# Transposing V as 32-bit words: four FP32 transposes per PSUM bank in place of eight BF16 ones, in the backward half of an attention block

## The chip, the cores and the metric

The kernel runs on one core of a Trainium2 chip. That core has five engines with their own instruction queues: TensorE (PE in the profile, with its weight loads shown as PEld), VectorE (DVE), ScalarE (ACT), GpSimd (POOL) and the queue that issues nearly all DMAs (SP). All DMAs share 16 DMA engines. The metric is the time of one execution in device microseconds, as a median of several runs.

## The reference, cut to what matters

The reference is one decode step of a transformer block and its gradients. Batch 4, 32 heads, 4096 cached positions, head size 128, so there are 128 (batch, head) pairs, called heads here; each head's K and V are 4096 x 128 BF16 values, 1 MB each.

```python
# forward: h = x + attention(layernorm(x)); out = h + swiglu(layernorm(h))
scores = jnp.einsum("bhqd,bhkd->bhqk", q, k_cache) * (Dh ** -0.5)
p = softmax(scores)
o = jnp.einsum("bhqk,bhkd->bhqd", p, v_cache)
# returned: out, and by jax.vjp the gradients of x, k_cache, v_cache, wq, wo, w1, w3, w2
```

For one head, with dO the gradient of o (128 values), the backward half needs three things:

- grad V, which is the outer product of p (4096) and dO (128): 1 MB written;
- dP, which is V times dO: 4096 numbers. This is the only use of V in the backward half, and V is read from memory a second time for it;
- dS = p * (dP - c) * scale, with c one number per head, and grad K, which is the outer product of dS and q: 1 MB written.

## The kernel before, in words

**Buffers.** SBUF holds an arena of 23 slots of 4160 BF16 values per partition. A slot holds one head's K, V, grad K or grad V, or a helper. Two adjacent slots hold a pair of heads. Which slot is given to what is decided when the program is written out, by the order of the calls and the ages of the slots, so it does not depend on the times. Every engine's instruction order is the order of the calls, written by hand (`manual_schedule`); only semaphores wait.

**Stages.** Up to about 690 us the forward half streams K and V once. Around 690 to 703 us lies a middle part with few heads' work (the gradient of the SwiGLU, then dO of the first eight head groups). Then come 32 single heads (`SP = 32`), and after them the other 96 heads as 48 pairs (`NT`). Each loop iteration calls `front` (V to dP), `more_V` (grad V, running ahead), `grad_K` or `grad_pair` (grad K) and `side` (a generator with the small gradients and dq). `front` runs L = 5 heads, or LP = 3 pairs, ahead of the grad K that needs its result.

**V to dP, single heads (`front`, L1214).** V lies in SBUF as 32 blocks j (one key each) of 128 values on each partition. A contraction over the 128 values of d needs d on the partitions, so V is transposed: per group g of eight blocks, TensorE writes eight 128 x 128 BF16 transposes into one PSUM bank (`V_T`, L800), and ScalarE copies the bank back over V (L801). Two such banks (`psT`) take turns. Then eight matmuls (L1230) with 512 moving columns each, four side by side on column strips of 32, multiply the transposed V with a stationary window of `zd`, a nearly empty tile with dO in one column; four heads share one PSUM tile `dP`, each writing its own rows. GpSimd places dO into `zd` two heads ahead (`dO_window`, L1195). After every fourth head, ScalarE copies dP out (`rows_out`, L1205), TensorE transposes it with four 128 x 128 FP32 transposes (`rows_T`, L1212), and VectorE forms dS (`group_dS`, L1247 and L1250).

**Pairs.** A pair's V is loaded as one 2 MB transfer. The first half of every partition's values goes through TensorE like a single head (`front_pair`, L1322, L1323, matmuls L1337, dO placed by `dO_pair`, L1292, into `zt`). The second half is transposed on VectorE in 32 x 32 blocks of 32-bit words (`rest_pair`, L1343), and its matmuls (L1349) read every second BF16 value, since a word holds two neighbouring d. Their stationary comes from `dO_quad` (L1312, GpSimd). `group_dS_pair` makes dS of four heads from both halves (L1359 to L1372).

**Outer products and stores.** VectorE makes each outer product (L806 for one head, L1424 for a pair), and the SP queue stores it (L817, L1257, L1434). `P_pairs` (L1200) and `P2_pair` (L1421) on GpSimd copy p into doubled form for them. SP also issues the V loads (L833 single, L1282 pairs), in program order, each waiting for its slot.

Of the kernel before, what the change touches and what calls it, by code (L numbers as in the profile page):

```python
# [9 lines left out]
FP32 = mybir.dt.float32  # L10
BF16 = mybir.dt.bfloat16
# [10 lines left out]
SP = 32  # L22
# [5 lines left out]
def kernel(  # L28
# [22 lines left out]
    nc = tc.nc  # L51
# [740 lines left out]

    def V_T(s, ps, part=range(SJ // GW)):
        if s not in VTs:
            VTs[s] = V2s.pop(s)
        v = VTs[s].heads()
        for g in part:
            pt = ps.tile([P, GW, P], BF16, tag="tps", name="pt_tps")
            for i in range(GW):
                nc.tensor.transpose(pt[:, i, :], v[:, g * GW + i, :], ident_b[:])  # L800
            nc.scalar.copy(out=v[:, g * GW:(g + 1) * GW, :], in_=pt[:])  # L801
# [163 lines left out]
    with ExitStack() as c2:  # L965
# [221 lines left out]
        zd = [bw3.tile([P, 136], BF16, name=f"zd{i}", tag=f"zd{i}", bufs=1) for i in range(B)]  # L1187
        dOp = bw3.tile([P, 4, (NH - SP) // 2], BF16, name="dOp", tag="dOp", bufs=1)
        quads = bw3.tile([P, 4], BF16, name="quads", tag="quads", bufs=1)
        for i in range(B):  # L1190
            nc.gpsimd.memset(zd[i][:], 0.0)

        def dO_window(s):
            if s < SP:
                nc.gpsimd.tensor_copy(out=zd[s % B][:, 32:132:67], in_=dOT_bf[:, s:s + 1].to_broadcast([P, 2]))  # L1195
# [18 lines left out]
        def front(s):  # L1214
# [8 lines left out]
            VT = VTs[s].heads()  # L1223
# [3 lines left out]
            for u in range(2):  # L1227
                for c in range(4):
                    j0 = 8 * c + 4 * u
                    nc.tensor.matmul(rows["acc"][32 * c:32 * (c + 1), :], lhsT=zq_window(zd[hl], 2 * hl + u),  # L1230
                                     rhs=VT[:, j0:j0 + 4, :], start=(hl == 0 and u == 0),
                                     stop=(hl == B - 1 and u == 1), tile_position=(0, 32 * c))
# [8 lines left out]
        def group_dS(g):  # L1241
            i0 = g * B
            T = rows.pop("T").rearrange("p jj (c m) -> p c m jj", c=4)
            t = rows.pop("t")[:, 0:B * SJ].rearrange("p (b j) -> p b j", b=B)
            t5 = t.rearrange("p b (c u jj) -> p b c u jj", c=4, u=2)
            for hl in range(B):
                nc.vector.tensor_scalar(out=t5[:, hl], in0=T[:, :, 2 * hl:2 * hl + 2, :], scalar1=c_rep[:, i0 + hl:i0 + hl + 1],  # L1247
                                        scalar2=scale, op0=ALU.subtract, op1=ALU.mult)
# [40 lines left out]
        def dO_pair(t):  # L1289
            if t < NT:  # L1290
                s, s2 = two(t)
                nc.gpsimd.tensor_copy(out=zt[t % B][:, 32:34], in_=dOT_bf[:, s:s2 + 1:B])  # L1292

        def dO_quads():
# [11 lines left out]
            for z in zd:  # L1306
                nc.gpsimd.memset(z[:], 0.0)

        def dO_quad(t):
            if t < NT:  # L1310
                for k in range(2):
                    nc.gpsimd.tensor_tensor(out=zd[2 * (t % 2) + k][:, 3:131].rearrange("p (q c) -> p q c", c=32)[:, :, 16:24:4],  # L1312
# [3 lines left out]
        def front_pair(t, mid):  # L1316
            pl = t % 2
            v = pV[t].t[:, 0:2 * SJ * Dh].rearrange("p (j d) -> p j d", d=Dh)
            for g in range(SJ // GW):
                pt = psT.tile([P, GW, P], BF16, tag="tps", name="pt_tps")  # L1320
                for i in range(GW):
                    nc.tensor.transpose(pt[:, i, :], v[:, g * GW + i, :], ident_b[:])  # L1322
                nc.scalar.copy(out=v[:, g * GW:(g + 1) * GW, :], in_=pt[:])  # L1323
# [9 lines left out]
            for u in range(2):  # L1333
                m = 4 * pl + 2 * u
                for c in range(4):
                    j0 = 8 * c + 4 * u
                    nc.tensor.matmul(rows["acc"][32 * c:32 * (c + 1), :], lhsT=zt[t % B][:, 32 - m:64 - m], rhs=v[:, j0:j0 + 4, :],  # L1337
                                     start=(pl == 0 and u == 0), stop=False, tile_position=(0, 32 * c))

        def rest_pair(t):  # L1340
# [4 lines left out]
            for g in range(2):  # L1345
                for r in range(2):
                    for k in range(2):
                        z0 = 3 + 4 * k - 2 * pl - g
                        nc.tensor.matmul(rows["acc"][:], lhsT=zd[2 * pl + r][:, z0:z0 + P], rhs=v5[:, 16 * g:16 * (g + 1), r, :, k],  # L1349
# [6 lines left out]
        def group_dS_pair(g):  # L1356
            T = rows.pop("T").rearrange("p jj (c z l u a) -> p z l a c u jj", c=4, z=4, l=2, u=2, a=2)
# [4 lines left out]
            t5 = t[:, :, 0:SJ].rearrange("p l (c u jj) -> p l c u jj", c=4, u=2)  # L1362
            t4 = t[:, :, SJ:2 * SJ].rearrange("p l (g j) -> p l g j", g=2)
            for l in range(2):
                for a, s in enumerate(two(2 * g + l)):
                    r_ = slice(64 * a, 64 * (a + 1))
                    nc.vector.tensor_scalar(out=t5[r_, l], in0=T[r_, 0, l, a], scalar1=c_rep[r_, s:s + 1],
                                            scalar2=scale, op0=ALU.subtract, op1=ALU.mult)
                    nc.gpsimd.tensor_scalar(out=t4[r_, l], in0=R[r_, 16 + 2 * l:18 + 2 * l], scalar1=c_rep[r_, s:s + 1],  # L1369
# [4 lines left out]

        Pp, zt, P2b, dSt = {}, [], [], []
# [4 lines left out]
        def P_rows(q):  # L1380
            if q >= NT // B or q in Pp:
                return
            if not Pp:
                Pp["s"] = Slot("Pp")
                x = Pp["s"].t[:, NT * 2 * SJ:]
                zt.extend(x[:, 66 * i:66 * (i + 1)] for i in range(B))
                nc.gpsimd.memset(x[:, 0:66 * B], 0.0)
                P2b.extend(x[:, n:n + 4 * SJ].rearrange("p (j t) -> p j t", t=2) for n in (66 * B, 66 * B + 4 * SJ))
                n = 66 * B + 8 * SJ
                dSt.append(x[:, n:n + 8 * SJ].bitcast(FP32))  # L1390
# [89 lines left out]

        for s in range(2):
            dO_window(s)
# [12 lines left out]
        for s in range(SP):  # L1495
# [11 lines left out]
            elif (s + L - SP) % 2 == 0:  # L1507
                if s + L == SP:
                    dO_pair(0)
# [66 lines left out]
```

## Time and profile before

| what | value |
|---|---|
| time, median of 3 runs (lowest to highest) | 1694.92 us (1694.87 to 1697.38) |
| the profiled execution: its own time | 1696.35 us |
| its span (first to last instruction) | 1694.5 us |
| mean granted TensorE clock | 0.832 of full speed |
| bytes moved by DMA | 707.25 MB, mean 417 GB/s |
| busy: DVE, PE, ACT, POOL | 80%, 71%, 46%, 32% |
| L800, BF16 transposes of single heads | 1024, 84.3 us busy |
| L1322, BF16 transposes of pairs | 1536, 160.6 us busy |
| copies of transposed banks (L801, L1323) | 128 of 1026 ns, 192 of 1024 ns |

A busy share is an average over stages that have different limits, so the stage must be looked at on its own. In a list of waits, a line names who waited, for whom, the sum in us, how often, and the longest. Times of matmuls overlap, since a matmul starts before the one ahead of it has ended: eight of 0.22 us can take 0.6 us together.

### The profile page before, as it was taken

Reading aid. Unit: us, or ns where it says so; the run is one execution under the profiler, and the core shown is the slowest. Engines: PE = TensorE matmul, PEld = TensorE weight load, DVE = VectorE, ACT = ScalarE, POOL = GpSimd, SP = SyncE. Lnnn points to the kernel's source line nnn. Section 1 sums busy time; section 2 is a strip of 40 time slices with the busy share of each in tenths; the row PEclk is TensorE's granted clock in tenths of the full one; section 3 lists DMA queues with packets and bytes.
Section 4 is the critical chain, followed back from the end, with each engine's and each line's share of the span. In section 5 each row is a group of like instructions: output and inputs, shape, how many; then the busy total and the mean of one; then the engine's idle time right before and its main releaser. Section 6 shows DMA issues by size and latency. Waiting matters only on the chain.

```text
span 1694.5 us, 34930 instructions
## 1 busy us (share of the span) xinstructions
PE 1204.6 (71%) x14708; PEld 859.8 (51%) x14708; DVE 1347.7 (80%) x1271; ACT 780.1 (46%) x1300; POOL 538.5 (32%) x779
## 2 busy tenths in 40 slices
PE   5989888888888888878886746656565575575550
PEld 4777766677676766656664533433232333233230
DVE  5999899999999997667767779698677687587585
ACT  3455444454455544677764333434342443344330
POOL 1211223222222222223331436454353345154110
PEclk9999999999999999799879668776667666656675
DMA  9999999999999999999999999999999999999997
GB/s 402 424 424 424 424 424 425 423 424 423 414 424 413 424 412 397 393 412 425 425 426 428 429 420 429 430 429 431 430 427 431 429 413 430 430 410 429 409 382 299
DMA packets 80988, 707.25 MB, mean 417 GB/s; under 512 B 8748, under 2 KB 12984, under 8 KB 15296
## 3 DMA queue, kind: packets, MB, share of 16 engines
q1 hardware_dynamic: 80416, 704.94, 99.1%
q8 instruction: 115, 1.88, 0.4%
q14 instruction: 41, 0.34, 0.0%
q0 software_dynamic: 416, 0.10, 0.0%
HBM read 422.59 MB, written 282.34 MB: 416 GB/s over the span
## 4 chain that ended last, share of the span: by engine, by line
DMA 35%; DVE 8%; ACT 4%; PE 4%; issue 3%; POOL 1%; DVEq 0%; SPq 0%; POOLq 0%; ACTq 0%
DMA out_dram<-arena 34%; DVE arena L1424 6%; ACT arena L801 4%; DMA arena<-in_A_v_cache_dram 2%; PE pt_tps L800 1%; DVE arena L1343 1%; PE dq_ps L1000 1%; PE dP_ps L1230 1%; DVE arena L806 1%; POOL arena L1369 1%; PE pt_wo L610 0%; DVEq L1571 0%; PE rep_ps L1179 0%; PE pt_tps L1322 0%; PE dP_ps L1349 0%
## 5 line engine op out<-in xcount | busy, mean ns | idle before, releaser
L472 PE MATMUL M_ps<-arena 128*128 128x130 bf16 x4096 | 284.7, 222 | 48.9 <-DMA arena<-in_A_v_cache_dram 48.4
L457 DVE TENSOR_TENSOR arena<-arena 128x4096 bf16<-128x4096 bf16 x128 | 292.4, 2284 | 23.5 <-POOL arena L453 23.5
L1323 ACT COPY arena<-pt_tps 128x1024 bf16<-128x1024 bf16 x192 | 186.2, 1024 | 245.5 <-PE pt_tps L1322 245.3
L1424 DVE TENSOR_TENSOR arena<-dS,arena 128x8192 bf16<-128x8192 bf16 x48 | 211.5, 4408 | 100.1 <-DMA out_dram<-arena 100.1
L472 PEld LDWEIGHTS <-arena 128*128 128x128 bf16 x4096 | 250.8, 99 | 70.9 <-DMA arena<-in_A_v_cache_dram 65.1
L1322 PE MATMUL pt_tps<-ident_b,arena 128*128 128x128 bf16 x1536 | 160.6, 280 | 157.2 <-DMA arena<-in_A_v_cache_dram 135.2
L1424 DVE TENSOR_TENSOR arena<-arena 128x8192 bf16<-128x8192 bf16 x48 | 212.2, 4421 | 57.3 <-DMA out_dram<-arena 57.3
L364 DVE STREAM_TRANSPOSE arena<-arena 128x512 f32<-128x512 f32 (+1 forms) x321 | 250.5, 797 | 0.0
L1312 POOL TENSOR_TENSOR zd<-dOp,quads 128x8 bf16<-128x8 bf16 x96 | 151.1, 1589 | 268.6 <-PE dP_ps L1349 266.5
L1322 PEld LDWEIGHTS <-arena 128*128 128x128 bf16 x1536 | 139.6, 130 | 188.1 <-DMA arena<-in_A_v_cache_dram 151.4
L359 ACT COPY arena<-pt_tps 128x1024 bf16<-128x1024 bf16 x128 | 129.4, 1012 | 194.1 <-PE pt_tps L358 154.9
L1349 PE MATMUL dP_ps<-arena,zd 128*128 128x512 bf16 x384 | 145.7, 545 | 83.4 <-DVE arena L1343 83.3
L453 POOL COPY arena<-P_all 128x64 bf16<-128x64 bf16 x128 | 32.4, 253 | 412.4 <-ACT P_all L447 409.4
L370 POOL TENSOR_TENSOR W<-qrep,wmask 128x128 bf16<-128x128 bf16 x128 | 119.5, 933 | 86.5 <-PE S_ps L390 71.7
L801 ACT COPY arena<-pt_tps 128x1024 bf16<-128x1024 bf16 x128 | 122.1, 1026 | 30.4 <-PE pt_tps L800 28.8
L1349 PEld LDWEIGHTS <-zd 128*128 128x128 bf16 x384 | 45.5, 123 | 164.3 <-issue 149.4
L978 ACT CAST arena<-gps 128x512 bf16<-128x512 f32 x110 | 60.5, 585 | 124.4 <-PE gps L984 124.4
L1343 DVE STREAM_TRANSPOSE arena<-arena 128x2048 f32<-128x2048 f32 x48 | 110.5, 2301 | 0.7 <-DMA arena<-in_A_v_cache_dram 0.7
L800 PE MATMUL pt_tps<-ident_b,arena 128*128 128x128 bf16 x1024 | 84.3, 240 | 24.1 <-ACT arena L801 23.9
L1421 POOL COPY arena<-arena 128x128 bf16<-128x128 bf16 x48 | 70.2, 1462 | 67.4 <-ACT arena L1398 63.0
L800 PEld LDWEIGHTS <-arena 128*128 128x128 bf16 x1024 | 72.9, 110 | 34.7 <-issue 33.2
L806 DVE TENSOR_TENSOR arena<-dS,arena 128x4096 bf16<-128x4096 bf16 x32 | 72.9, 2285 | 16.3 <-DMA out_dram<-arena 16.1
(256 smaller groups left out, 1891.3 us busy)
## 6 DMA issues: line engine op xcount, KB each, us to landing
out_dram<-arena SPq DMA_DIRECT2D x96, 2048.0 KB, 27.7
arena<-in_A_v_cache_dram SPq DMA_DIRECT2D x160, 1024.0 KB, 16.1
arena<-in_A_k_cache_dram SPq DMA_DIRECT2D x128, 1024.0 KB, 15.7
arena<-in_A_v_cache_dram SPq DMA_DIRECT2D x48, 2048.0 KB, 27.0
out_dram<-arena SPq DMA_DIRECT2D x72, 1024.0 KB, 20.1
arena<-in_A_wq_dram SPq DMA_DIRECT2D x8, 1024.0 KB, 14.4
arena<-in_B_w_dram SPq DMA_DIRECT2D x8, 896.0 KB, 14.4
out_dram<-arena SPq DMA_DIRECT2D x6, 896.0 KB, 27.8
```

The source lines that it names most:

```text
L359: nc.scalar.copy(out=KT[:, c * GW:(c + 1) * GW, :], in_=pt[:])
L364: nc.vector.transpose(out=KT[:, c * w_:(c + n) * w_], in_=Kn[:, c * w_:(c + n) * w_])
L457: nc.vector.tensor_tensor(out=PK[:, :, 0:Dh].rearrange("p j (r t) -> p j r t", t=2), in0=Ks[s].heads().rearrange("p j (r t) -> p j r t", t=2),
L472: nc.tensor.matmul(hold["M"][:], lhsT=Vn[:, j, :], rhs=PK[:, j, :], start=(j == 0), stop=(j == SJ - 1))
L800: nc.tensor.transpose(pt[:, i, :], v[:, g * GW + i, :], ident_b[:])
L801: nc.scalar.copy(out=v[:, g * GW:(g + 1) * GW, :], in_=pt[:])
L1312: nc.gpsimd.tensor_tensor(out=zd[2 * (t % 2) + k][:, 3:131].rearrange("p (q c) -> p q c", c=32)[:, :, 16:24:4], in0=dOp[:, None, 2 * k:2 * ...
L1322: nc.tensor.transpose(pt[:, i, :], v[:, g * GW + i, :], ident_b[:])
L1323: nc.scalar.copy(out=v[:, g * GW:(g + 1) * GW, :], in_=pt[:])
L1343: nc.vector.transpose(out=v.bitcast(FP32), in_=v.bitcast(FP32))
L1349: nc.tensor.matmul(rows["acc"][:], lhsT=zd[2 * pl + r][:, z0:z0 + P], rhs=v5[:, 16 * g:16 * (g + 1), r, :, k], start=False, stop=(pl == 1 ...
L1424: nc.vector.tensor_tensor(out=dst.rearrange("p (j r t) -> p j r t", r=Dh // 2, t=2), in0=col2[:, :, None, :].to_broadcast([P, 2 * SJ, Dh / ...
```

## The change

V is no longer transposed value by value in BF16. Its memory is read as 32-bit words, each holding two neighbouring d of one key. Two adjacent blocks j make 128 words, so one 128 x 128 FP32 transpose turns two blocks: `words_T` issues four per bank where eight BF16 ones were issued, and ScalarE copies the bank as before. After it, partition 64 i + r holds word r of block i of each couple (d = 2r and 2r + 1), and along the free dimension the two d of a word lie side by side. So the dP matmuls read every second BF16 value (`words_of`, k chooses the even or the odd d), and one matmul handles both blocks of a couple: the stationary has dO's even (or odd) values on partitions 0 to 63 in the column of block 0, and again on partitions 64 to 127 in the column of block 1. The number of these matmuls and their 512 columns stay.

That layout of dO is made by `dO_words`: four small matmuls and one ScalarE copy, once ahead of the single heads and once ahead of the pairs. `dO_window` and `dO_pair` now place it with two GpSimd copies of 64 partitions where one copy of 128 was. The order of the rows of dP changes, so `group_dS` and `group_dS_pair` read the transposed dP with the two inner dimensions exchanged. The VectorE half of each pair stays as it is. In the two programs' instruction streams, SP's are the same instruction for instruction, and VectorE's have the same instructions with only that read pattern changed.

```diff
+    def words_T(ps, v, g):
+        w = v.bitcast(FP32).rearrange("p (x r) -> p x r", r=Dh)
+        pt = ps.tile([P, GW, P], BF16, tag="tps", name="pt_tps")
+        ptw = pt.rearrange("p a b -> p (a b)").bitcast(FP32).rearrange("p (x q) -> p x q", q=P)
+        for jj in range(4):
+            nc.tensor.transpose(ptw[:, jj, :], w[:, 4 * g + jj, :], ident_f[:])
+        nc.scalar.copy(out=v.rearrange("p (j d) -> p j d", d=Dh)[:, g * GW:(g + 1) * GW, :], in_=pt[:])
+
+    def words_of(v, g, k):
+        return v.rearrange("p (x r t) -> p t x r", r=Dh, t=2)[:, k, 4 * g:4 * g + 4]
+
     def V_T(s, ps, part=range(SJ // GW)):
...
-            pt = ps.tile([P, GW, P], BF16, tag="tps", name="pt_tps")
-            for i in range(GW):
-                nc.tensor.transpose(pt[:, i, :], v[:, g * GW + i, :], ident_b[:])
-            nc.scalar.copy(out=v[:, g * GW:(g + 1) * GW, :], in_=pt[:])
+            words_T(ps, VTs[s].t[:, 0:SJ * Dh], g)
...
+        zd = [z[:, 0:64].rearrange("p (k c) -> p k c", k=2) for z in zq_]
+        dOw = dOp[:, 0:2, 0:SP]
...
+        def dO_words(dst, s0, s1):
+            ps = psrep.tile([P, 2, s1 - s0], FP32, tag="rep", name="dOw_ps")
+            for k in range(2):
+                for i in range(2):
+                    nc.tensor.matmul(ps[64 * i:64 * (i + 1), k, :], lhsT=ident_b[:, k:P:2], rhs=dOT_bf[:, s0:s1],
+                                     start=True, stop=True, tile_position=(0, 64 * i))
+            nc.scalar.copy(out=dst, in_=ps[:])
+
         def dO_window(s):
             if s < SP:
-                nc.gpsimd.tensor_copy(out=zd[s % B][:, 32:132:67], in_=dOT_bf[:, s:s + 1].to_broadcast([P, 2]))
+                for i in range(2):
+                    r_ = slice(64 * i, 64 * (i + 1))
+                    nc.gpsimd.tensor_copy(out=zd[s % B][r_, :, 2 * (s % B) + i], in_=dOw[r_, :, s])
...
-            for u in range(2):
+            for k in range(2):
                 for c in range(4):
-                    j0 = 8 * c + 4 * u
-                    nc.tensor.matmul(rows["acc"][32 * c:32 * (c + 1), :], lhsT=zq_window(zd[hl], 2 * hl + u),
-                                     rhs=VT[:, j0:j0 + 4, :], start=(hl == 0 and u == 0),
-                                     stop=(hl == B - 1 and u == 1), tile_position=(0, 32 * c))
+                    nc.tensor.matmul(rows["acc"][32 * c:32 * (c + 1), :], lhsT=zd[hl][:, k, :], rhs=words_of(v, c, k),
+                                     start=(hl == 0 and k == 0), stop=(hl == B - 1 and k == 1), tile_position=(0, 32 * c))
...
-            T = rows.pop("T").rearrange("p jj (c m) -> p c m jj", c=4)
+            T = rows.pop("T").rearrange("p jj (c m) -> p c jj m", c=4)
...
         def dO_pair(t):
             if t < NT:
                 s, s2 = two(t)
-                nc.gpsimd.tensor_copy(out=zt[t % B][:, 32:34], in_=dOT_bf[:, s:s2 + 1:B])
+                for i in range(2):
+                    r_ = slice(64 * i, 64 * (i + 1))
+                    nc.gpsimd.tensor_copy(out=zt[t % B][r_, :, ZP + 2 * i:ZP + 2 * i + 2], in_=zt[B][r_, :, s - SP:s2 - SP + 1:B])
...
         def front_pair(t, mid):
...
-                for i in range(GW):
-                    nc.tensor.transpose(pt[:, i, :], v[:, g * GW + i, :], ident_b[:])
-                nc.scalar.copy(out=v[:, g * GW:(g + 1) * GW, :], in_=pt[:])
+                words_T(psT, v, g)
...
-                    nc.tensor.matmul(rows["acc"][32 * c:32 * (c + 1), :], lhsT=zt[t % B][:, 32 - m:64 - m], rhs=v[:, j0:j0 + 4, :],
-                                     start=(pl == 0 and u == 0), stop=False, tile_position=(0, 32 * c))
+                    nc.tensor.matmul(rows["acc"][32 * c:32 * (c + 1), :], lhsT=zt[t % B][:, k, ZP - 4 * pl:ZP - 4 * pl + 32],
+                                     rhs=words_of(v, c, k), start=(pl == 0 and k == 0), stop=False, tile_position=(0, 32 * c))
...
+        dO_words(dOw, 0, SP)
         for s in range(2):
             dO_window(s)
...
                 if s + L == SP:
+                    dO_words(zt[B], SP, NH)
                     dO_pair(0)
                     dO_pair(1)
```

## The prediction

> **What bounds the kernel now.** I read the slices first, to see whether one resource is full all the time, then the busy times by stage, then the waits.
>
> The page's slices (40 of 42.4 us): DMA busy share in tenths, and the rate.
>
> ```profile
> DMA  9999999999999999999999999999999999999997
> GB/s 402 424 424 424 424 424 425 423 424 423 414 424 413 424 412 397 393 412 425 425 426 428 429 420 429 430 429 431 430 427 431 429 413 430 430 410 429 409 382 299
> ```
>
> The DMA engines are full in every slice but the last. The edited code starts in slice 16 (about 690 us). There the rate is low for two slices (397, 393), then about 425 in the single-head stage and 430 in the pair stage. The kernel can only end earlier where these rates sag.
>
> Busy time by stretch (columns: length, then busy us of PE, PEld, DVE, ACT, POOL with instruction counts, clock, DMA share, GB/s), for the single heads, the pairs and two places where the rate sags:
>
> ```profile
> 700.00:710.00 10.00, 6.57 (x55) 4.45 (x55) 7.97 (x6) 6.13 (x8) 4.30 (x13) 0.66 0.89 369
> 720.00:730.00 10.00, 7.29 (x84) 4.75 (x84) 6.77 (x9) 7.49 (x10) 4.15 (x5) 1.00 0.99 369
> 741.08:860.02 118.94, 96.88 (x1070) 73.28 (x1070) 83.70 (x68) 84.70 (x96) 36.88 (x34) 0.90 1.01 425
> 1200.00:1300.00 100.00, 58.29 (x401) 30.94 (x398) 71.56 (x35) 37.16 (x51) 41.77 (x35) 0.67 1.01 429
> ```
>
> The single heads run with DMA share 1.01 and PE busy 81%; the pairs with DMA 1.01 and PE 58%. No engine is full.
>
> The waits from 700 us to the end, longest first (who waited for whom; sum, times, longest):
>
> ```profile
> POOL zd L1312 <- PE dP_ps L1349: 266.5, 64, 20.3
> ACT arena L1323 <- PE pt_tps L1322: 245.3, 75, 13.2
> DVE arena L1424 <- DMA out_dram<-arena: 157.5, 35, 13.4
> PEld L1322 <- DMA arena<-in_A_v_cache_dram: 151.4, 36, 10.2
> ```
>
> In the pair stage PE waits for V to land and DVE waits for stores to free slots: both wait for DMA. DVE's waits for PE are few: 9.4 us in all for the transposed dP (L1247) and 8.9 us for dO columns (L775), both among the single heads.
>
> **The transposes.** Removed: 1024 + 1536 = 2560 BF16 transposes in 320 banks. Added: 1280 FP32 ones in the same 320 banks. The new operation is already in the trace: L1212 does four 128 x 128 FP32 transposes into a bank. It stands next to a bank of the old kind twice, once at full clock and once near 773 us, where the clock is lower:
>
> ```profile
> 722.54 0.61 PE L800 MATMUL pt_tps<-ident_b,arena 128*128 128x128 bf16 x8 [0.70 <-ACT arena L801]
> 723.03 0.66 PE L1212 MATMUL dPT_ps<-ident_f,dPr 128*128 128x128 f32 x4
> ...
> 771.97 1.01 PE L800 MATMUL pt_tps<-ident_b,arena 128*128 128x128 bf16 x8 [0.29 <-ACT arena L801]
> 772.78 1.06 PE L1212 MATMUL dPT_ps<-ident_f,dPr 128*128 128x128 f32 x4
> ```
>
> Four FP32 cost 0.66 us where eight BF16 cost 0.61, and 1.06 against 1.01. Half the instructions give no PE time back: 320 x 0.05 = 16 us more PE, over a stage of nearly 1000 us. Each bank's ScalarE copy is the same instruction as before (1.02 us) and is longer than the bank's transposes at full clock, so of four banks only the first one of a head lies on the path, 0.05 us.
>
> **The dP matmuls** keep number and columns (256 of L1230, 384 of L1337), but read every second value. The nearest row is the forward half's L390, where one strip reads dense K (the zq rows) and three read every second value (the W rows), 256 columns each, at full clock. Its starts: 302.10, 302.21, 302.32, 302.43 dense, and 302.11, 302.22, 302.35, 302.48 strided, so 0.11 us against 0.12 per step. For 512 columns that is 0.02 us per step, 0.04 per head. The lower end is 0; for the upper end I let the read rate halve. L482, eight such matmuls in two steps, takes 0.62 us, so halving adds 0.62 per head. I take 0.04, since L390 is the same kind of matmul.
>
> **GpSimd.** 32 + 48 placements become 160 copies of half the partitions: 80 more. The groups by shape:
>
> ```profile
> L1292 POOL COPY arena<-dOT_bf 128x2 bf16<-128x2 bf16 x48 | 35.1, 732 | 1.3
> L1195 POOL COPY zd<-dOT_bf 128x2 bf16<-128x2 bf16 x32 | 29.7, 933 | 39.7 <-PE dP_ps L1230 39.6
> ```
>
> At these means the addition is 48 x 0.73 + 32 x 0.93 = 65 us of POOL. The work itself is 0.19 us (median of L1195); its longest is 2.26 us and that of L1292 is 4.38 us, about as long as a VectorE outer product (2.28 and 4.42 us) that runs meanwhile. Lower end 80 x 0.19 = 15 us, upper 32 x 2.26 + 48 x 4.38 = 283 us. POOL is busy 42 of 100 us at 1200 us, and 65 us over 970 lifts that by 7 points, so I put it at nothing on the path. Behind a placement in POOL's queue stand the P copies (L1200, L1421) that VectorE's next outer product needs; VectorE waits for those at most 1.6 + 0.3 us in the trace. The cover is the DMA backlog: a pair's store lands 27.7 us after its issue, though 2 MB at 430 GB/s take 4.9. If it is gone, a late P copy costs its length.
>
> [...]
>
> **ScalarE, VectorE, waits.** ScalarE gains two small copies, VectorE none; `group_dS` reads the same 32 values per instruction in another order, and L1247 (0.72 us for four) is in the cover. PE gains 70 separate wait instructions, POOL 33, each 17 ns where the trace shows such a row: about 2 us, spread.
>
> **What lies on the path.** First the start of the single heads, where the DMA share is 0.89. Two banks of `V_T(0)` stand before the c matmul (L784) that releases POOL: +0.1. POOL places two heads before the first dP: two more copies in a row that took 0.31 us, +0.3. The four `dO_words` matmuls fall into the 2.54 us that PE waited for `zd` at 703 us: 0. Five fronts until the first dS (L1247 at 723.8 us), each 0.05 + 0.04, give +0.5. Sum +0.9. The lower end is 0 (DVE waited 3.16 us for this dS, but other stores were in flight); the upper end adds one blocked copy, 2.26, so 3.2. I take half of 0.9, since in the row at 720 us the DMA share is 0.99: +0.5.
>
> Second, the instructions themselves are fetched by DMA: 1.88 + 0.34 MB on the instruction queues. The streams shrink from 33,831 to 30,193 instructions (PE 28,539 to 24,785), so by 0.24 MB, at 417 GB/s -0.6 us.
>
> Third, the end. From 1598.6 us VectorE works nearly without a pause until 1676, then the last stores drain. PE's last dP transposes (L1212) end at 1651.9 and VectorE takes them at 1660.5; 0.3 us more of PE does not reach it: 0.
>
> Sum 1696.35 + 0.5 - 0.6 = 1696.25. The profiled execution is 1.43 us above the median, so for the median I write 1694.8.
>
> **Rivals.**
>
> Slower, by the front's pace. In the window above 17 heads pass in 118.94 us, 7.00 us each. DMA moves 3.15 MB per head (V in, two gradients out), 7.40 us at 425 GB/s. So the chain of PE and ACT is only 0.40 us per head from being the bound; that is where this decides. If strided reads halve the rate (+0.62) and every bank shows (4 x 0.05 = +0.20), a head takes 7.82, 0.42 too long; over the 27 heads after the first five that is 11.3 us: 1706. Against it: L390's pace. Chance 0.13.
>
> Slower, by GpSimd. P copies queue behind blocked placements and VectorE runs late near the sags: some four outer products of 2.28 us at the start, 9 us: 1704. For it: the 2.26 and 4.38 us rows; against it: the 1.9 us of waits. Chance 0.08.
>
> Faster. Halved instruction counts let PE answer sooner (34.5 us of "issue" before PEld L1322) where DMA sags: 690 to 730 (369, 369, 406, 369 against 425: 4.4 us), 1360 to 1380 (396, 404 against 430: 1.4) and 1480 to 1500 (408, 385: 1.6). All of it is 7.4 us: 1687.5; half is 1691. Against it: four FP32 are no shorter than eight BF16. Chance 0.15.
>
> That FP32 transposes run as fast as single BF16 ones (0.3 us less per bank, 96 us of PE) would not move the end either, since DMA is full; it belongs to "same".
>
> **How the numbers follow.** No change (within 0.2%, 3.4 us, about what a measurement of this kernel can tell) has 0.64, faster 0.15, slower 0.13 + 0.08 = 0.21. By itself the likeliest case spans 1691.5 to 1698.3. The range reaches down to 1688, nearly all of the faster case, and up to 1706, the price of the pace case, which takes in the GpSimd case too; some 1.2 in 10 is left out, mostly above.
>
> **What would show it.** The FP32 bank: four in 0.66 us at full clock; PE busy total near 1220 us against 1204.6. dP matmuls: eight in no more than 0.1 us above now. POOL busy near 600 us against 538.5. Rates of 425 and 430 in the two stages, and the DVE wait for stores near 157 us. It is wrong if VectorE's waits for the transposed dP (L1247's, 9.4 us before) grow several times, if PE no longer waits for V, or if VectorE waits for P copies.

## The result

The changed kernel takes 1689.18 us (median of 6 runs, 1688.03 to 1690.19) where the kernel before took 1695.33 (6 runs beside it, 1694.87 to 1697.38). The ratio is 0.9963, with a 95% interval of 0.995 to 0.9976: it is faster, by 6.2 us or 0.37%. The predicted range (1688 to 1706) holds the time, but the case called likeliest, "no change", does not.

### The profile page after: what moved, and what is told of

It is laid out like the page before. It is cut to its first block, busy times and chain, and to the rows that moved or that the text cites. A ratio compares the mean times of both kernels' runs of the same rounds, so it can differ in the third digit from the quotient of the medians.

```text
span 1688.4 us, 32572 instructions
## 1 busy us (share of the span) xinstructions
PE 1222.5 (72%) x13436; PEld 846.3 (50%) x13436; DVE 1348.3 (80%) x1271; ACT 781.9 (46%) x1302; POOL 591.1 (35%) x859
## 2 busy tenths in 40 slices
DMA packets 80980, 707.12 MB, mean 419 GB/s; under 512 B 8748, under 2 KB 12984, under 8 KB 15296
## 3 DMA queue, kind: packets, MB, share of 16 engines
q8 instruction: 106, 1.74, 0.4%
## 4 chain that ended last, share of the span: by engine, by line
DMA 36%; DVE 8%; PE 8%; ACT 5%; issue 3%; POOL 1%; DVEq 0%; SPq 0%; POOLq 0%; ACTq 0%
DMA out_dram<-arena 28%; DMA arena<-in_A_v_cache_dram 9%; DVE arena L1442 6%; ACT arena L799 4%; PE pt_tps L798 2%; DVE arena L1357 1%; POOL arena L1383 1%; PE dP_ps L1248 1%; PE dP_ps L1363 1%; PE M_ps L472 1%; DVE arena L457 1%; PE pt_w L601 1%; PE dq_ps L1007 1%; PE pt_wo L610 0%; ACT Pn L436 0%
## 5 line engine op out<-in xcount | busy, mean ns | idle before, releaser
L798 PE MATMUL pt_tps<-ident_f,arena 128*128 128x128 f32 x1280 | 257.1, 356 | 171.1 <-DMA arena<-in_A_v_cache_dram 125.5
L798 PEld LDWEIGHTS pt_tps<-ident_f,arena 128*128 128x128 f32 x1280 | 193.9, 184 | 230.6 <-issue 127.1
L472 PEld LDWEIGHTS <-arena 128*128 128x128 bf16 x4096 | 251.7, 99 | 67.3 <-DMA arena<-in_A_v_cache_dram 61.4
L1331 POOL TENSOR_TENSOR zd<-dOp,quads 128x8 bf16<-128x8 bf16 x96 | 160.7, 1691 | 241.9 <-PE dP_ps L1363 241.6
L1311 POOL COPY arena<-arena 64x4 bf16<-64x4 bf16 x96 | 103.7, 1080 | 30.6 <-ACT arena L1208 26.9
L358 PE MATMUL pt_tps<-ident_b,arena 128*128 128x128 bf16 x1024 | 80.5, 223 | 0.0
L482 PE MATMUL kP_ps<-arena,onesw 128*32 128x512 bf16 x1024 | 79.3, 386 | 0.0
L813 DVE TENSOR_TENSOR arena<-P,arena 128x4096 bf16<-128x4096 bf16 x29 | 66.3, 2292 | 16.0 <-DMA out_dram<-arena 15.2
```

The source lines that it names most:

```text
L472: nc.tensor.matmul(hold["M"][:], lhsT=Vn[:, j, :], rhs=PK[:, j, :], start=(j == 0), stop=(j == SJ - 1))
L798: nc.tensor.transpose(ptw[:, jj, :], w[:, 4 * g + jj, :], ident_f[:])
L813: nc.vector.tensor_tensor(out=dst.rearrange("p j (r t) -> p j r t", t=2), in0=col2[:, :, None, :].to_broadcast([P, SJ, Dh // 2, 2]), in1=r ...
L1331: nc.gpsimd.tensor_tensor(out=zq_[2 * (t % 2) + k][:, 3:131].rearrange("p (q c) -> p q c", c=32)[:, :, 16:24:4], in0=dOp[:, None, 2 * k:2 ...
```

## The profile after, beside the one before

First the page of the changed kernel: busy times, then the DMA rate in 40 slices, then the queue on which instructions are fetched (packets, MB, share).

```profile
PE 1222.5 (72%) x13436; PEld 846.3 (50%) x13436; DVE 1348.3 (80%) x1271; ACT 781.9 (46%) x1302; POOL 591.1 (35%) x859
...
DMA  9999999999999999999999999999999999999997
GB/s 402 424 424 424 424 424 424 424 424 423 414 423 413 423 410 400 395 409 425 425 426 428 430 431 429 430 429 431 430 428 432 430 424 428 424 417 432 426 390 305
...
q8 instruction: 106, 1.74, 0.4%
```

Two of these lines from the page of the kernel before (the slices stand in the prediction):

```profile
PE 1204.6 (71%) x14708; PEld 859.8 (51%) x14708; DVE 1347.7 (80%) x1271; ACT 780.1 (46%) x1300; POOL 538.5 (32%) x779
...
q8 instruction: 115, 1.88, 0.4%
```

PE's busy time went up (1204.6 to 1222.5 us) and the kernel still became faster. In the first 18 slices (up to 760 us) the rates are those of before within 3 GB/s. The difference lies behind them, mostly where the rate had sagged: the 24th slice has 431 where it had 420, the 33rd 424 for 413, the 36th 417 for 410, the 38th 426 for 409, the 39th 390 for 382; only the 35th went down by more than 2, from 430 to 424.

Busy time by stretch, changed kernel, the same four stretches that the prediction shows:

```profile
700.00:710.00 10.00, 6.82 (x38) 4.21 (x38) 7.39 (x6) 6.09 (x9) 6.43 (x17) 0.66 0.86 351
720.00:730.00 10.00, 7.09 (x52) 4.21 (x51) 6.89 (x9) 7.43 (x9) 5.40 (x9) 1.00 0.98 365
741.08:860.02 118.94, 95.91 (x798) 66.63 (x797) 83.03 (x66) 84.07 (x97) 49.31 (x50) 0.91 1.01 425
1200.00:1300.00 100.00, 60.42 (x312) 32.17 (x312) 70.94 (x39) 37.51 (x52) 41.60 (x44) 0.65 1.01 430
```

The start of the single heads is no better (351 and 365 against 369 and 369), and the two full stretches are at 425 and 430, as before. What fills up in part are the dips in between. The same view for five dips in the kernel before:

```profile
1000.00:1020.00 20.00, 14.90 (x136) 9.37 (x136) 18.84 (x12) 11.96 (x14) 16.47 (x16) 0.85 1.00 412
1360.00:1380.00 20.00, 13.69 (x103) 7.91 (x106) 18.97 (x11) 11.92 (x17) 12.95 (x15) 0.72 1.00 400
1480.00:1500.00 20.00, 16.64 (x89) 8.18 (x88) 18.97 (x11) 8.38 (x13) 12.43 (x10) 0.50 0.99 397
1600.00:1620.00 20.00, 11.36 (x82) 4.92 (x82) 18.96 (x12) 6.94 (x11) 4.17 (x8) 0.75 0.90 367
1640.00:1660.00 20.00, 8.99 (x46) 4.30 (x44) 20.00 (x7) 4.44 (x5) 0.69 (x2) 0.59 0.86 365
```

and in the changed kernel:

```profile
1000.00:1020.00 20.00, 13.03 (x102) 7.96 (x101) 18.48 (x11) 12.06 (x14) 17.98 (x17) 0.93 1.01 427
1360.00:1380.00 20.00, 14.83 (x71) 7.23 (x72) 19.40 (x6) 10.95 (x16) 11.20 (x12) 0.67 1.01 418
1480.00:1500.00 20.00, 15.61 (x66) 8.36 (x66) 18.96 (x11) 11.75 (x16) 13.16 (x12) 0.57 1.01 412
1600.00:1620.00 20.00, 14.69 (x69) 6.91 (x67) 17.00 (x10) 7.71 (x11) 10.30 (x12) 0.67 0.97 387
1640.00:1660.00 20.00, 3.97 (x12) 1.40 (x11) 18.97 (x11) 0.59 (x1) 1.68 (x4) 0.60 0.95 401
```

The last number of each line is the rate. The five differences (15, 18, 15, 20 and 36 GB/s) times 20 us at 430 GB/s make 0.7 + 0.8 + 0.7 + 0.9 + 1.7 = 4.8 us. This is a rough sum, since the two kernels drift apart inside the windows and the other windows of 20 us up to 1660 us differ by up to 8 GB/s either way, but it says where most of the time came from.

The same is seen transfer by transfer. SP issues the same transfers in the same order in both kernels, so each landing can be set beside its counterpart (us, after minus before, from the records of the two traces):

```
landing near   700    855    905    990   1070   1215   1354   1408   1480   1517   1555   1585   1631..end
difference     0.1   -0.85  -1.05  -1.65  -1.9   -2.5   -3.0   -3.5   -3.8   -4.1   -4.3   -5.3   -5.8
```

The gain is no single jump. It grows through the whole backward half, 0.6% of the time that passes there, with steps at the dips.

The waits from 700 us to the end, changed kernel:

```profile
ACT arena L799 <- PE pt_tps L798: 275.7, 115, 12.5
POOL zd L1331 <- PE dP_ps L1363: 241.6, 60, 18.5
DVE arena L1442 <- DMA out_dram<-arena: 151.4, 34, 13.1
...
PE pt_tps L798 <- DMA arena<-in_A_v_cache_dram: 125.5, 32, 10.1
```

They have the pattern of before: PE still waits for V, VectorE for stores to free its slots (157.5 before, 151.4 now). So both still wait for DMA, and the question is why DMA delivers the same bytes (707.12 MB against 707.25) in less time.

## The experiments

All theories have to explain a kernel that is full of DMA and yet reacts to PE's instructions. Theory F: PE's instructions are themselves a load on the DMA side, so fewer of them let the transfers land earlier. Rivals: A, PE answers sooner where DMA sags; L, the new layout, the GpSimd copies or the new places of small buffers do it. In the trace each of these matmuls and transposes has two rows, a weight load (PEld) and the matmul (PE). The change took out 1272 of 14708 such pairs of rows. All gains in us below are 1696 x (1 - ratio); a ratio's interval is worth about +/-2 us.

### Idle matmuls added to the changed kernel

```diff
+        zero = bw3.tile([P, 16], BF16, name="zero", tag="zero", bufs=1)
+        nc.gpsimd.memset(zero[:], 0.0)
...
         for g in range(2):      # rest_pair, the VectorE half of a pair
+                if g == 1:
+                    for _ in range(64):       # 32 in the second kernel
+                        nc.tensor.matmul(rows["acc"][0:16, 0:4], lhsT=zero[:], rhs=v[:, 0:4], start=False, stop=False)
```

The third kernel has `range(5)` and 512 moving columns (`rows["acc"][0:16, 0:512]`, `v[:, 0:512]`): much PE time in few instructions.

> The changed kernel (1689.2 us) with 64 idle matmuls added to each pair's second half: a zero stationary of 16 columns, 4 moving columns, added to the dP tile, so nothing computed changes. That is 64 x 2 x 48 = 6144 more PE rows (matmul and weight load). Fetch theory (the gain of 6.15 us is that 2544 fewer PE rows are fetched by DMA, 2.4 ns each; the instruction queue q8 of before, 0.4% of 16 engines for 115 packets of 256 instructions, gives about 0.94 us a packet or 3.7 ns each if one DMA engine carries it): 15 to 22 us more, 1704 to 1711. q8 has some 24 packets more. Answer theory (the gain is PE answering sooner where DMA sags): about 1.8 us of PE per pair, of which PE's waits for V take most: 1689 to 1693. Layout theory (the gain is in dO's placement and the read order): 1689.

Measured: 1696.51 us against 1696.45, ratio 1.0 (0.9991 to 1.0009). The gain is gone.

> As the run with 64, with 32 idle matmuls per pair: 3072 more PE rows. Fetch theory: half of the other's addition, 7.4 to 11 us, 1696.5 to 1700.5, so about before's time or above it. Answer theory: 1689 to 1691. Layout theory: 1689.

Measured: 1693.23, ratio 0.998 (0.9971 to 0.9989). Half of the gain is gone.

> The changed kernel with 5 idle matmuls of 512 moving columns per pair instead of many tiny ones: about 5 x 0.33 = 1.6 us of PE per pair, near that of the 64 tiny ones, but only 480 more PE rows. Fetch theory: 1.2 to 1.8 us more, 1690.4 to 1691. Answer theory: as much as the run with 64 tiny ones, and no less than that with 32.

Measured: 1690.93, ratio 0.9967 (0.9954 to 0.9979). Nearly all of the gain is kept.

Reading: 3072 idle matmuls cost 6.7 us and 1536 cost 3.3 us against the changed kernel (mean ratio of its two measurements 0.996), so 2.2 ns for each, in proportion. The 240 wide ones raised PE's busy time by 34 us and cost about 1 us. That alone does not decide between PE's time and the number of its instructions, since the 64 raised the busy time too, by 105 us (1222.5 to 1327.3): by time the wide ones would cost 2.1 us, by number 0.5, and both lie within the interval. The changed kernel itself has 18 us more PE time and is faster, and two runs further down (`half_pairs` and `bf16_in_bank`) speak against PE's time. Also, 2.2 ns x 1272 explains only 2.8 of the 6.2 to 7.1 us gained, and the expectation for the 64 was two to three times too high. The price per fetched packet is no constant either: the 64 added 24 packets of 16 KB for 6.7 us, the change took out 9 for as much.

### Half the transposes, without the new layout

```diff
-            for i in range(GW):
-                nc.tensor.transpose(pt[:, i, :], v[:, g * GW + i, :], ident_b[:])
-            nc.scalar.copy(out=v[:, g * GW:(g + 1) * GW, :], in_=pt[:])
+            for i in range(GW // 2):
+                nc.tensor.transpose(pt[:, i, :], v[:, g * GW + 2 * i, :], ident_b[:])
+            nc.scalar.copy(out=v[:, g * GW:(g + 1) * GW, :].rearrange("p (a b) d -> p a b d", b=2),
+                           in_=pt[:, 0:GW // 2, None, :].to_broadcast([P, GW // 2, 2, P]))
```

The cut shows one of two places; the same edit stands in the pairs' `front_pair`.

> The kernel before (1695.3 us) with BF16 transposes of only every second block: four per bank, and ScalarE copies each of the four twice, so its copy has the same size. Half of V is left out of dP, so dP is not the reference's. It has the PE rows of the changed kernel's transposes (2560 fewer than before), but before's dO placement, dense reads and row order, and a bank's transposes take about half of 0.61 us. Fetch theory: 1689 to 1690. Answer theory: below the changed kernel, about 1685, since its banks are 0.3 us shorter. Layout theory: 1695.

Measured: 1695.09, ratio 0.9997 (0.9988 to 1.0006). The single heads' stage explains this. Busy time of this kernel between 740 and 860 us:

```profile
740.00:860.00 120.00, 100.80 (x674) 67.31 (x674) 76.74 (x59) 73.45 (x84) 49.25 (x32) 0.53 1.01 405
```

and VectorE's two longest waits for PE between 690 and 1000 us:

```profile
DVE dPr L1248 <- PE dPT_ps L1213: 40.5, 8, 11.8
DVE dOT_bf L775 <- PE dOT_ps L773: 24.3, 3, 13.9
```

The granted clock is 0.53 in that stretch, where it was 0.90 before. At that clock PE is busier with less work, the front falls behind, the wait for the transposed dP is 40.5 us where it was 9.4, and DMA falls to 405 GB/s. Between 1000 and 1035 us its landings were about 7 us later than before; from there to the end it made up about 8.5 us and ended 1.45 us ahead. So this run does not test the theory in the single heads. It looks like the pace case of the prediction, brought about by the clock, and it points at a gain in the pairs alone. (Not all of the 8.5 us is the pairs': `half_pairs` below, with the same code in that stage, made up 5.7 us there.) That was the reason for the next four.

### The two stages apart

`pairs_only` gives the single heads back their BF16 code of before; `singles_only` does so for the pairs, with the old places of the small buffers; `half_pairs` is the kernel before with the edit above in `front_pair` alone (its TensorE half of each pair).

> The changed kernel as it is, on the chip and in the call of the three next ones, so that their parts can be added up. All theories: 0.9963 of the time before, 6.2 us less.

Measured: 1689.09 against 1696.9, ratio 0.9958 (0.9946 to 0.9971): 7.1 us.

> The single heads' V is transposed as before (eight BF16 per bank, one placement of dO per head); only the pairs take the FP32 words. 768 of the 1280 transposes are gone, which is 1536 of the 2544 PE rows (weight load and matmul). If the time goes with the number of PE rows at the 1.0 ns per row that the added idle matmuls measured, the gain is 1.5 us (0.9991). If the whole gain of 6.2 us goes with the rows removed, it is 3.7 us (0.9978). If it comes from something that only the pairs have (the other places of the small buffers, with the copies of p at 0.38 us where they took 1.46), it is 4 to 6 us (0.9964 to 0.9976).

Measured: 1691.41, ratio 0.9968 (0.9955 to 0.998): 5.4 us.

> The reverse: FP32 words for the 32 single heads, the pairs as before, their small buffers at the old places. 512 transposes, 1024 PE rows less. By 1.0 ns per row: 1.0 us less (0.9994). By the rows' share of the whole gain: 2.5 us less (0.9985). If the gain is the pairs' alone: 0 (1.0).

Measured: 1694.2, ratio 0.9985 (0.9976 to 0.9994): 2.5 us.

> The kernel before, where in the pairs' TensorE half only every second block of V is transposed (four BF16 per bank) and ScalarE copies each twice into place; the other blocks of V are left out of dP, so grad K and grad x's attention part aren't the reference's. The single heads are as before. 768 BF16 transposes less, that is 1536 PE rows, with no FP32 transposes, no new layout of dO, no added GpSimd copies and the small buffers at their old places; PE's time falls by about 0.3 us per bank. By the number of PE rows alone it gains what the pairs alone gain. If that gain is the layout's or GpSimd's, this kernel gains only 1.5 us by 1.0 ns per row (0.9991); if PE's shorter answers count, it gains more than the pairs with FP32 words.

Measured: 1690.93, ratio 0.9962 (0.9949 to 0.9974): 6.4 us.

The page's busy times of `pairs_only`, then of `half_pairs`:

```profile
PE 1215.8 (72%) x13944; PEld 850.3 (50%) x13944; DVE 1348.3 (80%) x1271; ACT 781.1 (46%) x1301; POOL 572.8 (34%) x827
PE 1189.7 (70%) x13940; PEld 802.2 (47%) x13940; DVE 1348.1 (80%) x1271; ACT 778.6 (46%) x1300; POOL 553.5 (33%) x779
```

and a stretch of the pair stage of `half_pairs`:

```profile
1200.00:1300.00 100.00, 56.61 (x309) 24.47 (x308) 71.57 (x36) 36.90 (x51) 41.60 (x36) 0.62 1.01 429
```

`half_pairs` has as many PE instructions as `pairs_only` (13940 and 13944), but no FP32 transposes, the old layout of dO, the old GpSimd copies and 26 us less PE time (1189.7 against 1215.8). Both gain the same within their intervals. So in the pairs rival L falls, and rival A has no support: 26 us less PE time bought nothing that could be measured. Within their intervals the parts add up (5.4 + 2.5 = 7.9 against 6.2 and 7.1), and they go with the transposes taken out, 764 and 508: 7 and 5 ns for each. That is two to three times the price of the idle matmuls.

### Place or kind of the instruction

In the changed kernel, ahead of the four FP32 transposes of each bank of the pairs, into the bank that these overwrite:

```diff
+        for i in range(4):
+            nc.tensor.matmul(ptw[0:16, 0, 0:4], lhsT=zero[:], rhs=v[:, 4 * i:4 * i + 4], start=True, stop=True)   # tiny_in_bank
+            nc.tensor.transpose(pt[:, i, :], v[:, (8 * g + i) * Dh:(8 * g + i + 1) * Dh], ident_b[:])           # or: bf16_in_bank
```

`quarter_pairs` is `half_pairs` with every fourth block (`GW // 4`, `4 * i`, each copied four times).

> The changed kernel with four idle matmuls (zero weights of 16 columns, four moving columns) ahead of the four FP32 transposes of each bank of the pairs, into the bank that these then overwrite: 768 matmuls, 1536 PE rows more, at the place of the removed ones, and next to no PE time. If a PE row costs the same wherever it stands, the 1.0 ns of the rows added in one lump behind the pair's other half: 1.5 us above the changed kernel, 0.9968 to 0.9972 of before. If rows between V's landing and the bank's copy cost what taking them out of the pairs gained (5.5 to 6 us): 0.9992 to 1.0.

Measured: 1691.96, ratio 0.9973 (0.9963 to 0.9984): 2.1 us above the changed kernel, 2.7 ns for each of 768.

> The changed kernel with four BF16 transposes of V blocks ahead of the four FP32 ones of each bank of the pairs, overwritten by these: the same 1536 PE rows more, and 0.3 us more PE time per bank (192 banks). By 1.0 ns per row: 1.5 us above the changed kernel, 0.9968 to 0.9972. If what the change saved in the pairs was the transposes themselves as read and written by PE (their weight loads of V, their time): 5.5 to 6 us above it, 0.9992 to 1.0, while the run with the tiny matmuls stays at 0.997.

Measured: 1693.46, ratio 0.9984 (0.9975 to 0.9993): 4.0 us above it, 5.2 ns for each. This is where `singles_only` stands (0.9985), which has the same number of PE instructions (14204 and 14200) and none of the pairs' new layout.

> The kernel before with only every fourth block of V transposed in the pairs (two BF16 per bank, each copied four times into place by the same ScalarE copy); three quarters of those blocks are left out of dP. 1152 BF16 transposes, 2304 PE rows less than before, 768 rows less than where every second block was transposed. If the time goes on with the rows at that run's 4 us per 1000 rows: 9 us below before (0.9945). By 1.0 ns per row: 0.8 us below that run (0.9957). If its gain was a threshold (PE answering in time for the transfers) that is already passed: as that run, 0.9962.

Measured: 1688.69, ratio 0.9956 (0.9943 to 0.9968): 7.5 us below before. The three expected values (0.9945, 0.9957, 0.9962) all lie within the interval, so the run doesn't choose between them; it lies 1.1 us below `half_pairs`, within the noise.

The place matters little (2.7 ns against 2.2 in a lump elsewhere). A full BF16 transpose at this place costs about twice a tiny matmul, though the two intervals overlap. PE's time is hardly the reason: `bf16_in_bank` has 4 us more of it than the changed kernel (1226.5 against 1222.5) and lost 4.0 us, `wide5` has 34 us more and lost about 1.

### Full weight loads

```diff
+            for i in range(12):
+                nc.tensor.matmul(ptw[:, 0, 0:4], lhsT=v[:, (8 * g + i % 8) * Dh:(8 * g + i % 8 + 1) * Dh], rhs=ident_b[:, 0:4], start=True, stop=True)
```

> The changed kernel with twelve idle matmuls ahead of the FP32 transposes of each bank of the pairs: each loads a full 128 x 128 BF16 block of V as weights, as a BF16 transpose does, but multiplies only four moving columns, into the bank that the transposes then overwrite. 2304 matmuls, 4608 PE rows more. If a row costs what the tiny matmuls cost (1.0 to 1.5 ns wherever they stood): 4.7 to 7 us above the changed kernel, 0.999 to 1.0005 of before. If it is the full load of V as weights that made the BF16 transposes dearer (2.5 ns per row): 11 to 12 us above it, 1.003. PE has the room: 64% busy in the pairs, and each bank's transposes and loads stay beside ScalarE's copy of 1.02 us.

Measured: 1704.08 against 1695.42, ratio 1.0052 (1.0038 to 1.0066). That is 15.5 us above the changed kernel, 6.7 ns for each of 2304 matmuls: the price of a transpose, three times that of a matmul with 16 columns of zeros. The dips of this kernel, for comparison with the two lists above:

```profile
1360.00:1380.00 20.00, 18.09 (x166) 10.28 (x165) 18.95 (x11) 10.10 (x14) 13.23 (x15) 0.63 0.96 376
1480.00:1500.00 20.00, 14.94 (x108) 7.17 (x107) 18.95 (x12) 9.15 (x14) 8.71 (x10) 0.50 0.87 349
```

They are deeper than before the change (400 and 397). The expectation's cover did not quite hold, though. ScalarE's copies of banks, which should follow each other, now wait for PE:

```profile
1201.46 1.01 ACT L801 COPY arena<-pt_tps 128x1024 bf16<-128x1024 bf16 x1 [0.25 <-PE pt_tps L800]
1202.77 1.01 ACT L801 COPY arena<-pt_tps 128x1024 bf16<-128x1024 bf16 x1 [0.29 <-PE pt_tps L800]
```

About 0.8 us per pair, by three such gaps of 0.25 to 0.29 us, is added to the way from V to dP (an estimate). PE waits 123 us for V at the pairs in this run, 2.6 us per pair, so there is room for it, but a part of the 15.5 us may be this and not the weight loads.

### What the DMA records say

In the records each transfer lands in 16 parts. In the kernel before, 127 waits of PE, VectorE, ScalarE or GpSimd after 690 us are put down to a transfer, and each ended 0.02 to 0.22 us behind its last part. In the backward half the last part comes behind the 15th by a time that grows from stage to stage (before: 0.6 us at 740 to 860 us, 5.2 at 1000 to 1200, 12.05 at 1450 to 1600). Most 16 KB packets take 611 ns, some take 615 to 690 ns. Between 1100 and 1300 us, before and after, these follow one another: 97% of them begin no earlier than 20 ns before the end of the one ahead. The records do not name their engine. From the records (without `half`): matmul count, the gain, that stretching summed (each packet's time over the usual one of its size, up to 0.14 us, fetches left out; us per 100 us, 1100 to 1300 us), and the mean distance of the last part from the 15th (us, 1450 to 1600 us):

```
kernel            matmuls   gain    stretched   last part behind
weights_in_bank    15740    -8.8      3.18        14.6
bf16_in_bank       14204     2.7      2.29        12.2
before             14708     0        2.19        12.05
pad64              16508     0        2.55        11.4
pad32              14972     3.4      2.23        11.8
singles_only       14200     2.5      2.14        12.0
tiny_in_bank       14204     4.6      2.14        10.6
pairs_only         13944     5.4      1.81        10.6
half_pairs         13940     6.4      1.91        10.4
changed kernel     13436   6.3, 7.1  1.90, 1.92   9.8, 10.0
wide5              13676     5.6      2.02         9.2
quarter_pairs      13556     7.5      1.67         9.8
```

From kernel to kernel the stretching follows the instructions: 2.1 to 2.3 ns for each instruction that ran in that stretch in most of these kernels (before: 2.19 us x 2 for 2045 instructions), 1.5 to 1.8 in the two with the tiny matmuls in a lump. The change took 2358 instructions out of the trace; at 2.2 ns that is an estimate of 5.2 us, of 6.2 to 7.1 us gained, if all of it falls on one DMA engine and that engine's part lands last, which the records do not show. This is what theory F comes to. It is a correlation, not a proof: no run moved this load to another DMA engine.

Three things in the same records speak against a fixed price per instruction. In the kernel before, between 100 and 650 us, 18397 instructions ran in 550 us and the same sum is 0.6 ns for each, where between 1100 and 1300 us it is 2.2. `half` has few instructions between 1100 and 1300 us (1698) and more stretching than any kernel of the table (3.6 us per 100 us); its clock there is 0.58, hardly below the 0.61 of `half_pairs`, so the clock is no good reason to leave it out. And neither column orders the gains: `bf16_in_bank` is slightly above the kernel before in both and gains 2.7 us, `pad64` has the last part closer (11.4) and gains nothing. So the runs show that the number and kind of PE's instructions change the time; by what way they do is not shown.

Two things stay open. The first is what the load is. Instruction fetch is seen in the trace (packets of 16 KB on q8 that take 0.93 us in the median after 700 us; as one ends, from 1000 us on and in all but one case, a data packet of 16 KB begins that takes 0.96 to 1.16 us where 0.61 is usual), but the records don't show on which engines these fall, and the stretching is counted without them. Every timed execution here was also recorded by the profiler, so the recording itself, which leaves a row for each instruction, can't be excluded as the load. The second is why a full weight load costs two to three times a tiny one.

## Why the prediction was right and wrong

**The step that failed** is the second one on the path: "the instructions themselves are fetched by DMA ... -0.6 us". It had the right sign and looked in the right place, the number of PE's instructions (whether as work for DMA is not shown), but its size was wrong by a factor of ten. It took bytes at the rate of all 16 engines. Even in its own terms it was too high: the FP32 transposes have weight-load rows of their own in the trace (L798, PEld x1280), so the fetched bytes fell from 1.88 to 1.74 MB, which is 0.3 us at 417 GB/s. What the runs showed in its place is 5 to 8 ns for each 128 x 128 transpose taken out, 6.2 to 7.1 us in all. The likeliest case fell with it: a full DMA was taken as cover for whatever PE does, and the runs show that it is none for the number of PE's instructions.

The fetch itself is small in the page: 115 packets on q8 before and 106 after, 0.4% of the 16 engines in both. But 3072 idle matmuls cost 6.7 us, and 2304 with full weight loads 15.5 us, in a kernel whose PE was waiting for DMA (125.5 us for V in the changed kernel); whether through the fetch is open.

**The faster rival** had the sign, the sum and two of the places. Its price was 1687.5 to 1691 and the time is 1689.2. The sags at 1360 and 1480 us filled in part (400 to 418 and 397 to 412), but the start of the single heads (369 to 351 and 365), its largest item with 4.4 us, did not, and the dips at 1000, 1600 and 1640 us, which it did not name, rose. Its reason, PE answering sooner, isn't what the runs show: `half_pairs` with 26 us less PE time gains no more, clear of the noise, than `pairs_only`. The "issue" time that it started from can't be compared: the row ahead of the FP32 transposes' weight loads reads 127.1 us now, but in 28 of its 35 waits, 124.7 us, PE itself was waiting for V, which the view of before puts down to DMA. The stated range holds the time only because it was drawn down to take in this rival, which had a chance of 0.15 and a reason that the runs don't bear out; that part is luck.

**The transposes.** Right. PE's busy time rose by 17.9 us where 16 were worked out, 12 of them in the transposes themselves (84.3 + 160.6 before, 257.1 after), and the banks took what L1212's had shown (changed kernel, a clock of 1 and the lower clock):

```profile
722.95 0.66 PE L798 MATMUL pt_tps<-ident_f,arena 128*128 128x128 f32 x4 [0.67 <-ACT arena L799]
...
773.66 1.11 PE L798 MATMUL pt_tps<-ident_f,arena 128*128 128x128 f32 x4 [0.29 <-ACT arena L799]
```

**The dP matmuls.** Right; the strided reads cost almost nothing (42.5 and 44.1 us before):

```profile
L1351 PE MATMUL dP_ps<-arena 128*32 128x512 bf16 x384 | 46.6, 476 | 5.3 <-ACT arena L799 5.3
L1248 PE MATMUL dP_ps<-arena,zd 128*32 128x512 bf16 x256 | 42.6, 419 | 18.2 <-ACT arena L799 16.6 <-POOL zd L1214 1.5
```

With that the pace rival had no ground. Its margin looks real, though: in `half`, where the clock fell to 0.53, VectorE waited for this front and the rate fell to 405.

**GpSimd.** The sum near 600 us came out (591.1), but from two misses that in part cancel:

```profile
L1311 POOL COPY arena<-arena 64x4 bf16<-64x4 bf16 x96 | 103.7, 1080 | 30.6 <-ACT arena L1208 26.9
L1214 POOL COPY zd<-dOp 64x2 bf16<-64x2 bf16 x64 | 54.2, 847 | 32.4 <-PE dP_ps L1248 30.5
L1439 POOL COPY arena<-arena 128x128 bf16<-128x128 bf16 x48 | 18.0, 375 | 56.1 <-issue 27.2 <-ACT arena L1416 22.4 <-DVE arena L1442 4.3
```

The placements cost 157.9 us for 64.8, so 93 more and not 65, and the copies of p (L1421 before, 70.2 us, 1462 ns each) became 52 us cheaper. The two misses hang together, as a place near 1200 us shows, first before, then after:

```profile
1199.78 4.50 POOL L1421 COPY arena<-arena 128x128 bf16<-128x128 bf16 x1
...
1197.51 4.30 POOL L1311 COPY arena<-arena 64x4 bf16<-64x4 bf16 x1
1201.88 0.29 POOL L1439 COPY arena<-arena 128x128 bf16<-128x128 bf16 x1
```

Before, 14 of the 48 copies of p and 6 of the 48 placements of the pairs took over 1 us; after, 1 of 48 and 21 of 96. Each of these 42 overlaps an outer product of VectorE and ends 0.04 to 0.15 us after it, and the median copy of p takes 0.29 us in both kernels. So this wait for VectorE moved from the copy of p to the placement ahead of it in GpSimd's queue. None of it was on the path, as predicted; VectorE waited 0.4 us for a P copy, 0.3 before (the prediction's other 1.6 us was put down to a placement, L1195).

**The waits.** VectorE's wait for the transposed dP grew from 9.4 to 14.4 us, that for dO columns from 8.9 to 13.3, far from "several times". The start cost nothing visible (+0.5 us predicted; the landings were level at 700 us and 0.85 us earlier at 855), and the end added nothing of its own (-5.8 us from 1631 us on).

## What to carry to other kernels

This kernel was bound by DMA and still reacted to the mere number of instructions of an engine that waited for DMA (3072 idle matmuls cost 6.7 us): measure a price per instruction with idle ones (in this kernel 2 to 3 ns for a tiny matmul, 5 to 7 ns for a full 128 x 128 weight load with its matmul) before putting a change in their count at nothing. Look at the last of a transfer's 16 parts, not only at the mean busy share of the DMA engines: here a share of 1.00 (1450 to 1600 us, before) stood beside a last part that landed 12 us behind the 15th, and in `half` beside a rate of 405 GB/s instead of 425. And when a theory explains the sign, check its size with an edit that does only this one thing: half the transposes without the new layout gave the whole gain of the pairs, and the bytes of instruction fetch, at the rate of all 16 engines, explain less than a tenth of the change's gain.

## What the runs showed of the hardware that was not expected

- The last of a transfer's 16 parts falls behind the 15th, from 0.6 us at 740 to 860 us to 12 us at 1450 to 1600 us in the kernel before and to 14.6 us in `weights_in_bank`. Whether one DMA engine was slower is not shown.
- A granted TensorE clock of 0.53 instead of 0.90 in the single-head stage when only every second block was transposed (`half`), and of 0.90 again when the same edit was made in the pairs alone. Fewer matmuls (674 in 120 us for 1070 in 119) went with a lower clock there, and the DMA rate fell (425 to 405 GB/s). Why the clock fell is not known.
- None of the 63 GpSimd copies before and 61 after that began during a VectorE outer product (after 690 us) ended ahead of it, whatever their size: 4.50 us for a copy of p whose median is 0.29 us, 4.30 us for a placement of 64 x 4 values whose median is 0.19. Copies that were already running as one began (31 and 43) ended inside it. With a second placement ahead of the copy of p in the queue the wait moved (over 1 us before: 14 of 48 copies of p and 6 of 48 placements; after: 1 of 48 and 21 of 96).
